# The scales of the split units: sums of magnitudes on ScalarE in place of maxima on VectorE, an exponentials' table loaded first, and a new listed order

## The chip, the cores and the metric

One core of one Trainium2 chip runs the program. The metric is the device time of one execution in microseconds (us); lower is better. Times before and after are medians of several runs, and each version was also executed once with the hardware profiler.

Engines are named as in the profile: PE (TensorE, matmuls; PEld is its weight load), DVE (VectorE), ACT (ScalarE), POOL (GpSimd), SP (SyncE, which here issues all the DMAs).

## The reference

Attention with two kinds of masks, and then one feed-forward block over all tokens:

```
scores = q @ k^T / sqrt(64)                      # 8 batches, 8 heads, 576 positions
mask   = window of 32 (heads 0-3), or every 4th of 128 back (heads 4-7)
attn   = softmax(scores where mask, else -1e9)
x      = (attn @ v) as 4608 tokens x 512
h      = x @ w_in                                # 512 -> 2048
g      = h * tanh(softplus(h))                   # Mish
out    = g @ w_out                               # 2048 -> 512
```

All inputs and the output are float32.

## The kernel before

The work is cut into 16 units of 288 tokens: unit u is half u % 2 of batch u // 2. A unit is loaded (`loads`, `loads_v`), prepared (`prep`), attended in four pairs of heads (`scores_of_pair`, `scores`, `exps`, `transpose_p`, `values`), and goes through the two layers (`ff1` or, from unit 4 on in pairs of units, the seven products `s_p1` to `s_p7`; then `gate` and `ff2`).

To keep float32 accuracy with float16 products, numbers are split: a value, multiplied by a power of two, is written as a high float16 part and a low one that holds the rest, and three products are added up. The weights are split at the start (`w_load`, `w_max`, `w_scale`, `w_words`, `w_split`). Units 0 to 2 are "direct": their attention is in float32, and only v's maximum is needed. Units 3 to 15 are "split": q, k and v are split as well, and `prep` makes the powers of two for them.

For a split unit, `prep` has these steps (each `yield` ends one):

1. POOL clears `m` (L497), and DVE takes the maximum magnitude of each partition of q (`amax`, L327), then of the two k tiles, then of the two v tiles: five reductions into the columns of `m`.
2. `over_partitions` (L336): one PE matmul of `m` with ones, which gives every partition the same sum over the partitions of each column.
3. DVE joins pairs of columns (L516) and cuts the result to a power of two (`pow2_scales`, L321 to L323).
4. ACT scales q (L541), writes the high parts of q (L544), k (L548) and v (L564); POOL (L551) and DVE (L554, L568) subtract for the low ones.

[...] Exponentials (L689, L695) and Mish (L947, L1028) lie in different tables, so an ACT_TABLE_LOAD stands wherever the two follow each other.

Nothing is scheduled on the chip. `ORDER` is a list written out ahead, in which a name such as `pr3` is the next step of `prep(3)`, and a number behind it names the buffer or the PSUM bank that the step takes. The program runs through the list, and each engine gets its instructions in that order. The four banks (pairs of 512 columns in PSUM) are shared by all products. `kw` entries are matmuls of zeros (L1081) that keep PE at work while it has nothing else to do. `ol` (`open_late`) gives back the buffers of the weights' loading and takes others in their place, which POOL clears (L712, L714); `wf` (`w_forms`, L871 to L877 on POOL) makes combinations of the weights for the pairs of units; `mr` makes the masks (L305).

Of the kernel before, what the change touches and what calls it, by code (L numbers as in the profile page):

```python
# [45 lines left out]
tx0.1 tx0.1 wl0.2.1=1 va0.3=1 sp1.1=0 tp0.0=1 wp0.3.1 xa0.1=1 tp0.0=0 wp0.3.0 tx0.3=2 sc1.1=0 lv1 wp0.3.1 wp0.3.0 tx0.3
kw9=3 va0.0=1 va0.0 kw11=3 tx0.3 va0.0=0 sp1.0=0 sc1.0=2 wl0.1.1=0 tx0.3 wm0.2.1=0 ww0.2.1 va0.2=2 va0.2 ex1.0 va0.2=1
ws0.2=1 ws0.2 tx0.0=2 tx0.0 tx0.2=0 tx0.2 tx0.0 tx0.0 ww0.2.1 sp1.2=1 wm0.1.1=0 ww0.1.1 sp1.3=2 sc1.3=3 tx0.2 tx0.2
ff0.1=3 ff0.6=0 ff0.6 wl0.1.0=3 wm0.1.0=0 sc1.2=1 ww0.1.0 ww0.2.0 ws0.1=1 ws0.1 ff0.1 wp0.2.1 ex1.3 pr1 ex1.2 ww0.1.1
xa1.1=2 ex1.1 wp0.2.0 wp0.2.0 tp1.3=2 tp1.3=0 fs0 ff0.0=1 ff0.6=0 ld2 ff0.0 ff0.0=1 ff0.1 ff0.7=2 pr1=0 pr1 gt0.0=0  # L50
ff0.7 ff0.7 wp0.2.1 wp0.1.1 va1.3=1 ww0.1.0 tp1.0=0 tp1.0=1 va1.3 va1.3=0 tp1.1=2 tp1.1=0 wp0.1.1 kw8=3 va1.0=0 va1.0
wp0.1.0 va1.0=1 tp1.2=2 tp1.2=1 lv2 ff0.5=3 pr2 va1.1=1 tx1.3=2 tx1.3 ff0.4=0 ff0.4 xa1.0=3 gt0.3=1 va1.1 wl1.3.1=2
va1.1=0 wl1.2.0=1 wm1.2.0 wp0.1.0 ww1.2.0 pr2=1 gt0.3 ff0.4=2 tx1.3 tx1.3 ff0.5 tx1.0=0 pr2 wl1.2.1=0 ff0.2=2 wm1.2.1
tx1.0 tx1.1=1 tx1.0 ff0.2 ww1.2.1 wm1.3.1 ww1.3.1 tx1.1 tx1.1 tx1.0 va1.2=0 ws1.2=1 ff0.5 gt0.2=2 xa2.1=4 ww1.3.1
ff0.3=3 va1.2 va1.2=1 tx1.2=0 ff0.2=0 sp2.1=2 ws1.2 wl1.3.0=3 wm1.3.0 ww1.3.0 tx1.2 tx1.2 sc2.1=3 sp2.3=1 sc2.3=2 tx1.2
ex2.3 ws1.3=0 ws1.3 ex2.1 ff0.3 ww1.3.0 ff1.2=0 ff1.6=1 wp1.3.1 wp1.3.1 ww1.2.1 xa2.0=0 tp2.1=2 tp2.1=0 ff1.2 gt0.2
gt0.0 va2.1=2 ff0.3 wp1.3.0 wp1.3.0 wp1.2.1 wp1.2.1 ff1.6 ww1.2.0 ff1.7=3 ff1.7 fs1 ff1.6=2 ff1.2=1 ff1.7 gt1.3=3 va2.1
va2.1=0 wl1.0.1=2 wm1.0.1 gt1.3 ff1.3=1 ff1.3 ww1.0.1 ff1.3 tp2.3=0 sp2.2=3 gt0.1=4 gt0.1 tp2.3=1 sc2.2=0 ff1.1=1
wl1.0.0=3 gt1.1=5 ff1.0=2 ff1.0 wm1.0.0 ww1.0.0 wl1.1.0=0 ff1.1 ff1.0=2 wp1.2.0 gt1.1 ff1.1 va2.3=0 va2.3 ws1.0=2
wp1.2.0 ws1.0 ex2.2 wm1.1.0 sp2.0=1 sc2.0=1 va2.3=1 ex2.0 fo0.2.0=2 fo0.2.1 ww1.1.0 ww1.0.1 ff1.5=3 ff1.5 gt1.0=6  # L60
tx2.1=0 gt1.0 wl1.1.1=1 ff1.4=1 wm1.1.1 tx2.1 wp1.0.1 ff1.4 ff1.4=0 ff1.5 fs2 fo0.2.2 ww1.1.0 tx2.1 tx2.1 ww1.1.1
wf1.1=1 fo0.2.3 fo0.2.3=0 lv3 tp2.0=1 ww1.1.1 wp1.0.1 tp2.2=3 ww1.0.0 fo0.3.0 ws1.1=0 ws1.1 tp2.2=0 va2.2=3 tp2.0=1
va2.0=1 va2.0 va2.0=0 gt1.2=7 fo0.3.1 gt1.2 fo1.2.0=0 tx2.0=1 wp1.1.0 fo1.2.1 fo1.2.2 wp1.1.0 fo1.2.3 wp1.1.1 wp1.1.1
fo0.2.3 va2.2 va2.2=0 tx2.2=3 wp1.0.0 tx2.2 fo0.3.2 wp1.0.0 fo0.3.3 tx2.2 fo0.3.3=1 tx2.2 fo1.2.3=0 fo1.3.0 fo1.3.1
tx2.3=2 ol wf0.0=2 wf0.0 mr ld3 tx2.0 pr3 pr3 wf0.0=0 pr3 pr3=3 wf0.0 pr3 fo1.3.2 tx2.3 wf1.1 fo0.3.3 wf1.1=2 wf1.1
wf0.0 fo0.0.0=3 wf1.1 fo1.2.3 tx2.3 fo1.3.3 fo0.0.1 fo0.0.2 pr3 pr3 fo0.0.3 fo1.3.3=1 tx2.0 fo1.3.3 pr3 pr3 pr3 sp3.1=2
pr3 fo0.0.3=0 pr3 sp3.2=1 sc3.1=3 ex3.1 ld4 sp3.0=0 fo0.1.0 fo0.1.1 sc3.0=2 sc3.2=1 xw4.0=2 fo1.0.0=2 fo1.0.1 fo1.0.2
fo0.0.3 wf0.1=1 fo1.0.3 lv4 wf0.1 ex3.0 wf0.1=0 sp3.3=0 tp3.1=0 wf0.1 tp3.0=1 fo0.1.2 wf0.1 fo1.0.3=1 fo0.1.3 ff2.3=1
fo1.1.0 fo1.1.1 ex3.2 tp3.0 tp3.0=0 sc3.3=0 ex3.3 tp3.3=1 pr4 wf1.0=2 tp3.1 tp3.1=1 ff2.0=0 ff2.0 ff2.0=1 fo1.1.2
va3.0=0 pr4 pr4 fo0.1.3=0 wf1.0 xa3.1=1 pr4=3 pr4 ff2.3 wf1.0=0 wf1.0 fo0.1.3 wf1.0 fo1.1.3 tp3.3 fo1.1.3=0 ff2.5=3  # L70
# [1067 lines left out]
```

## Time and profile before

| | before |
|---|---|
| median of 3 timed runs | 885.92 us (885.57 to 889.34) |
| profiled execution | 883.43 us, its span 881.7 us |
| PE busy | 856.6 us (97%) |
| DVE busy | 682.4 us (77%) |
| ACT busy | 609.7 us (69%) |
| POOL busy | 190.2 us (22%) |
| granted PE clock, mean | 0.996 |

The span is the time from the first instruction to the last; the execution has 1.7 us around it. A busy share is an average over the span: stages with different limits lie in it. In the views, a row names the line, the engine, the operation, and what it writes and reads (out<-in); "idle before" is the time that the engine stood before it, and what ended it. A wait is put down to the event that came last.

### The profile page before, as it was taken

What the parts mean: (1) busy time and instruction counts of PE and PEld (TensorE: products, weight loads), DVE (VectorE), ACT (ScalarE), POOL (GpSimd) and SP (SyncE); (2) the same over time, 40 slices, a digit from 0 to 9 for tenths busy, and PEclk for the clock granted to TensorE, in tenths of its full rate; (3) what the DMA queues carried; (4) which work ended last, traced back from release to release, by engine and by line L of the source; (5) the groups of instructions that cost most, each with busy time, mean ns of one, the idle gap of its engine ahead of it and who ended that gap; (6) DMA issues with size and microseconds to landing.
All of it is one profiled execution on the core that took longest, in us unless ns stands there. A gap on an engine that the chain in (4) does not pass through costs nothing.

```text
span 881.7 us, 21314 instructions
## 1 busy us (share of the span) xinstructions
PE 856.6 (97%) x8920; PEld 689.4 (78%) x8924; DVE 682.4 (77%) x960; ACT 609.7 (69%) x853; POOL 190.2 (22%) x218
## 2 busy tenths in 40 slices
PE   9999996999999999999999999999999999999998
PEld 8687884778777778877888778877788778887776
DVE  6999995899998979669887899896987788633310
ACT  3787973566887689578976689748875688536521
POOL 1000106715445110351024010431024110220000
PEclk9999998999999999999999999999999999999999
DMA  7953432565788975766766777677867763655200
GB/s 239 307 185 114 153 123 71 169 157 114 186 168 196 219 199 154 166 158 207 201 142 140 220 185 168 136 170 199 205 132 178 182 204 70 134 114 188 97 25 31
DMA packets 210865, 141.20 MB, mean 160 GB/s; under 512 B 151376, under 2 KB 195920, under 8 KB 210768
## 3 DMA queue, kind: packets, MB, share of 16 engines
q1 hardware_dynamic: 210768, 139.83, 61.5%
q8 instruction: 70, 1.15, 0.5%
q14 instruction: 27, 0.22, 0.1%
HBM read 93.06 MB, written 16.78 MB: 125 GB/s over the span
## 4 chain that ended last, share of the span: by engine, by line
PE 56%; DVE 13%; ACT 4%; issue 3%; DMA 3%; POOL 1%; SPq 0%; DVEq 0%; ACTq 0%; POOLq 0%
PE b L1052 27%; PE b L937 24%; PE b L778 2%; DMA w<-wd 2%; PE b L624 2%; DVE m L327 2%; DVE g L1042 1%; DVE sb L648 1%; DVE sb L656 1%; DVE nm L654 1%; DVE p L739 1%; DVE w L922 1%; ACT k L548 0%; DVE w L796 0%; ACT p L737 0%
## 5 line engine op out<-in xcount | busy, mean ns | idle before, releaser
L1052 PE MATMUL b<-g,w 128*128 128x288 f16 x3072 | 391.5, 287 | 0.2 <-DVE xs L796 0.2
L1052 PEld LDWEIGHTS <-w 128*128 128x128 f16 x3072 | 297.7, 98 | 75.9 <-DVE xs L796 0.3
L937 PEld LDWEIGHTS <-w 128*128 128x128 f16 x2016 | 194.8, 98 | 52.3 <-DMA w<-wd 3.1
L937 PE MATMUL b<-xf,w 128*128 128x288 f16 x1440 | 210.3, 286 | 1.9 <-DMA w<-wd 1.9
L1066 ACT ACTIVATE y<-b,fo 128x288 f32<-128x288 f32 x60 | 44.2, 744 | 90.4 <-PE b L1052 66.7
L1042 DVE SCALAR_TENSOR_TENSOR g<-hm,sg,g 128x1152 f16<-128x1152 f32 x64 | 90.6, 1421 | 17.9 <-ACT g L1040 17.8
L1025 PE MATMUL b<-xf,w 128*128 128x288 f16 x768 | 99.1, 286 | 2.7 <-DVE xs L796 1.2
L1025 PEld LDWEIGHTS <-w 128*128 128x128 f16 x768 | 74.1, 98 | 22.8 <-issue 2.1
L551 POOL TENSOR_TENSOR q<-qn,q 128x288 f16<-128x288 f32 (+1 forms) x39 | 45.5, 1198 | 172.9 <-ACT q L544 172.9
L1040 ACT ACTIVATE g<-hm,sg 128x1152 f16<-128x1152 f32 x64 | 79.9, 1252 | 1.1
L947 ACT ACTIVATE hm<-hm,fs 128x576 f32<-128x576 f32 x72 | 54.2, 769 | 15.7 <-DVE hm L998 7.1
L937 PE MATMUL b<-w,w 128*128 128x288 f16 x288 | 64.3, 286 | 0.0
L695 ACT ACTIVATE sb<-sb,ln_p 96x768 f32<-96x768 f32 (+3 forms) x52 | 46.4, 895 | 17.3 <-DVE sb L656 17.0
L656 DVE TENSOR_TENSOR sb<-sb,nm 96x768 f32<-96x768 f32 (+4 forms) x64 | 56.6, 884 | 2.2
L739 DVE TENSOR_TENSOR p<-sb,p 96x768 f16<-96x768 f32 (+3 forms) x52 | 51.1, 984 | 4.0 <-ACT p L737 3.8
L654 DVE TENSOR_REDUCE nm<-sb 96x6 f32<-96x768 f32 (+4 forms) x64 | 48.8, 762 | 1.8
L922 DVE TENSOR_TENSOR w<-w,w 72x1024 f16<-72x1024 f32 (+3 forms) x27 | 29.4, 1092 | 22.3 <-ACT w L920 22.3
L778 PEld LDWEIGHTS <-pT 128*128 128x128 f16 (+3 forms) x1092 | 39.3, 98 | 3.2 <-issue 1.0
L737 ACT CAST p<-sb 96x768 f16<-96x768 f32 (+3 forms) x52 | 41.0, 793 | 0.6
L910 POOL TENSOR_TENSOR w<-xs,w 72x1024 f32<-72x1024 f32 (+1 forms) x6 | 12.9, 2145 | 128.4 <-DVE xs L796 128.4
L937 PE MATMUL b<-xg,w 128*128 128x288 f16 x288 | 39.2, 286 | 0.0
L871 POOL TENSOR_TENSOR hm<-w 128x1024 f32<-128x1024 f16 x8 | 18.8, 2345 | 93.1 <-DVE g L1042 79.9
(173 smaller groups left out, 1194.8 us busy)
## 6 DMA issues: line engine op xcount, KB each, us to landing
w<-wd SPq DMA_DIRECT2D x84, 512.0 KB
qn<-in_qT SPq DMA_DIRECT2D x16, 576.0 KB
out_T<-y SPq DMA_DIRECT2D x64, 144.0 KB
raw<-in_w_in SPq DMA_DIRECT2D x16, 512.0 KB
raw<-in_w_out SPq DMA_DIRECT2D x16, 512.0 KB
vn<-in_v SPq DMA_DIRECT2D x48, 128.0 KB
wd<-hm SPq DMA_DIRECT2D x32, 128.0 KB
knd<-in_kdT SPq DMA_DIRECT2D x16, 208.0 KB
```

The costliest lines, as they stand in the source:

```text
L551: nc.gpsimd.tensor_tensor(lo, x, hi, op=ALU.subtract)
L654: nc.vector.tensor_reduce(nm[:nq, :, j:j + n], x, axis=AX.X, op=ALU.max, negate=True)
L656: nc.vector.tensor_tensor(blocked(sb, c0, n, w), x, nm[:nq, :, j:j + n].unsqueeze(3).broadcast_to([nq, 2, n, w]), op=ALU.add)
L695: nc.scalar.activation(x, x, AF.Exp, bias=ln_p[:nq])
L739: nc.vector.tensor_tensor(lo, src, hi, op=ALU.subtract)
L778: nc.tensor.matmul(avv[:, h, j], pp[:nk, c:c + P], vv[vi][:nk, j, hh, :], start=(i == 0), stop=(i == 2))
L937: nc.tensor.matmul(o[:, h, :HT], t[:, c, wi, h * P:(h + 1) * P], form_of(p, x, c, xi), skip_group_check=True, start=start and n == 0, stop ...
L947: nc.scalar.activation(o, src, AF.Mish, scale=U[2 * p]["fs"][:, j:j + 1])
L1025: nc.tensor.matmul(ph[:, h, :HT], w1[j][c // WIDE][:, c % WIDE, wi, k * P:(k + 1) * P], x_of(d, xi, c), start=(n == 0), stop=(n == len(seq ...
L1040: nc.scalar.activation(g[:, 0], m, AF.Identity, scale=sg)
L1042: nc.vector.scalar_tensor_tensor(g[:, 1], m, sg, g[:, 0], ALU.mult, ALU.subtract)
L1052: nc.tensor.matmul(po[:, :HT], w2[:, e, j, wi, k * P:(k + 1) * P], d["g"][j][:, gi, k, :], start=(j == 0 and n == 0), stop=(j == NCH - 1 a ...
```

## The change

Four things are different.

- `prep` of a split unit no longer takes maxima. `magnitudes` runs on ACT: the function Abs over the tile, divided by 1024, with the sum along the row put out (`accum_out`). The values themselves go to a place that is written later anyway (the high halves of q, k and v). A sum of magnitudes is no smaller than the largest, so it bounds the values as well.
- The sum over partitions by one matmul is replaced by `largest`: PE transposes the six columns, DVE takes the maximum of each row, DVE sets the six on the diagonal of a small matrix, and PE multiplies it with ones. This puts two PE steps in a unit's preparation where there was one. `m` is float32 for split units, and `pow2_scales` gets other constants.
- An exponential of one column is the first thing that ACT does, so its table is loaded ahead of everything else.
- `ORDER` is a new list (2355 entries; 2329 before): 26 more steps for the 13 split units, and the others in another sequence. `kw` has 249 matmuls of zeros in all, 269 before; ahead of the first weights' scales 136, before 226.

```
+MANY = 1024.0
...
-kw16=0 kw16=0 kw16=0 kw16=0 kw16=0 kw16=0 kw16=0 kw16=0 kw16=0 kw16=0 kw16=0 kw16=0 kw16=0 kw2=0 ws0.0=0 ws0.0 wp0.0.0
...
-    def pow2_scales(m, f, s):
+    def pow2_scales(m, f, s, tiny=TINY, by=2.0 ** -SPLIT_EXP):
...
-        nc.vector.tensor_scalar(f, f, TINY, 2.0 ** -SPLIT_EXP, ALU.max, ALU.mult)
+        nc.vector.tensor_scalar(f, f, tiny, by, ALU.max, ALU.mult)
...
+    def magnitudes(o, i, unused):
+        nc.scalar.activation(unused, i, AF.Abs, scale=1.0 / MANY, accum_out=o)
+
+    def largest(m, n, u):
+
+        t = single(u)[:n, :P]
+        nc.tensor.transpose(t, m[:, :n], ident)
+        yield
+        top = pool.tile([8, 1], F32, name="top", bufs=3)
+        nc.vector.tensor_reduce(top[:n], t, axis=AX.X, op=ALU.max)
+        on_diagonal = pool.tile([8, 8], BF16, name="dg", bufs=3)
+        nc.vector.tensor_scalar(on_diagonal[:n, :n], ident[:n, :n], top[:n], None, ALU.mult)
+        yield
+        o = single(u)[:, :n]
+        nc.tensor.matmul(o, ones_b[:n].broadcast_to([n, P]), on_diagonal[:n, :n], start=True, stop=True)
+        yield
+        return o
...
-        m = pool.tile([P, 6], BF16, name="m", bufs=3)
+        m = pool.tile([P, 6], BF16 if d["direct"] else F32, name="m" if d["direct"] else "mm", bufs=3)
...
-        amax(m[:, 4:5], qn)
+        magnitudes(m[:, 4:5], qn, q2[:, 0])
...
-            amax(m[:, 2 + i:3 + i], x)
+            magnitudes(m[:, 2 + i:3 + i], x, k2[:, 0, ksl[i]])
...
-        for x, o in ((vn, m[:, 0:1]), (vdn[:kd], m[:kd, 1:2])):
-            amax(o, x)
+        for x, o, y in ((vn, m[:, 0:1], vh[:, 0]), (vdn[:kd], m[:kd, 1:2], vdh[:kd, 0])):
+            magnitudes(o, x[:, :, :, :D].rearrange("p j h d -> p (j h) d"), y[:, :, :, :D].rearrange("p j h d -> p (j h) d"))
...
-        mr = yield from over_partitions(m, 6, u)
+        mr = yield from largest(m, 6, u)
...
-        pow2_scales(m3, f, s)
+        pow2_scales(m3, f, s, TINY / MANY, MANY * 2.0 ** -SPLIT_EXP / 2)
...
+    first = const.tile([P, 1], F32, name="first")
     with tc.manual_schedule(engines=None):
+        nc.scalar.activation(first, ln_p, AF.Exp)
```

How the new list moves instructions shows at three places. The first is the start, on DVE: `raw` is a weight tile as loaded, `w` its place, and `wm` the maximum that the first scales are made of. Before:

```order
L409 TENSOR_SCALAR w_125<-w_125 128x1024
L411 SCALAR_TENSOR_TENSOR raw_76<-raw_76,w_125 128x1024
L412 SCALAR_TENSOR_TENSOR raw_76<-raw_76 128x1024
L409 TENSOR_SCALAR w_119<-w_119 128x1024
L411 SCALAR_TENSOR_TENSOR raw_77<-raw_77,w_119 128x1024
L412 SCALAR_TENSOR_TENSOR raw_77<-raw_77 128x1024
L409 TENSOR_SCALAR w_118<-w_118 128x1024
L411 SCALAR_TENSOR_TENSOR raw_78<-raw_78,w_118 128x1024
L412 SCALAR_TENSOR_TENSOR raw_78<-raw_78 128x1024
L384 TENSOR_REDUCE wm_417<-b_72 128x1
```

After (line numbers are those of the changed kernel, 20 higher here):

```order
L429 TENSOR_SCALAR w_119<-w_119 128x1024
L431 SCALAR_TENSOR_TENSOR raw_76<-raw_76,w_119 128x1024
L432 SCALAR_TENSOR_TENSOR raw_76<-raw_76 128x1024
L429 TENSOR_SCALAR w_118<-w_118 128x1024
L431 SCALAR_TENSOR_TENSOR raw_77<-raw_77,w_118 128x1024
L432 SCALAR_TENSOR_TENSOR raw_77<-raw_77 128x1024
L404 TENSOR_REDUCE wm_323<-b_72 128x1
```

Two weight tiles stand ahead of the first scales instead of three. The second place is POOL where unit 3, the first split unit, begins: `p` and `pT` are tiles that `open_late` takes, `hm` a working tile of the weight forms, `m_d` and `m_r` the masks, and `m` (now `mm`) the columns of `prep(3)`. Before:

```order
L712 MEMSET p_1982 96x2048
L714 MEMSET pT_1984 128x1328
L871 TENSOR_TENSOR hm_140<-w_118 128x1024
L874 TENSOR_TENSOR hm_140<-hm_140 128x256
L875 TENSOR_TENSOR hm_140<-hm_140 128x256
L876 TENSOR_TENSOR hm_140<-hm_140 128x256
L877 TENSOR_TENSOR hm_140<-hm_140 128x256
L305 COPY m_d<-m_s 72x288
L305 COPY m_d<-m_s 72x416
L305 COPY m_r<-m_r 96x384
L497 MEMSET m 128x6
```

After:

```order
L732 MEMSET p_1906 96x2048
L734 MEMSET pT_1908 128x1328
L517 MEMSET mm 128x6
L891 TENSOR_TENSOR hm_139<-w_118 128x1024
L894 TENSOR_TENSOR hm_139<-hm_139 128x256
```

The clearing of unit 3's columns moved ahead of the weight forms and of the masks. The third place is the same one on the engine that goes over unit 3's tiles. On DVE before, from the last weight split (`w` from `raw` and its scale `ws`) to the columns' join:

```order
L424 SCALAR_TENSOR_TENSOR w_126<-raw_79,ws_1571,w_126 128x512 x2
L1058 TENSOR_SCALAR fo<-h_o,f 128x1 x2
L1064 TENSOR_SCALAR y_88<-b_72,fo 128x288
L327 TENSOR_REDUCE m<-qn 128x1
L327 TENSOR_REDUCE m<-knp 128x1
L327 TENSOR_REDUCE m<-knd 128x1
L327 TENSOR_REDUCE m<-vn 128x1
L327 TENSOR_REDUCE m<-vdn 104x1
L883 TENSOR_TENSOR hm_138<-hm_140,hm_138 128x1024
L516 TENSOR_REDUCE m_2026<-b_75 128x3
```

On ACT after, behind the last weight part:

```order
L1048 ACTIVATE hm_139<-b_72,fs 128x576
L844 CAST xf_133<-b_75 128x4x72
L1060 ACTIVATE g_162<-hm_139,sg 128x1152
L849 CAST xf_133<-b_75 128x4x72
L844 CAST xf_136<-b_73 128x288
L844 CAST xf_133<-b_72 128x4x72
L901 CAST hm_138<-hm_140 128x1024
L1086 ACTIVATE y_89<-b_74,fo 128x288
L345 ACT_TABLE_LOAD
L345 ACTIVATE q_1916,mm<-qn 128x1152
L345 ACTIVATE k_1931,mm<-knp 128x640
L345 ACTIVATE k_1931,mm<-knd 128x832
```

The passes over unit 3's tiles moved from DVE to ACT, with a table load ahead of them: the Mish passes just before (L1048) had their own table in place. The passes over v's two tiles follow. In the whole program the new order has 60 table loads for 44, and 11 of them stand directly ahead of magnitudes.

More of the change, by code (lines that the diff above doesn't have):

```diff
@@ L46 @@
[L46 to L70, printed above, removed]
@@ L186 @@
[L186 to L189 removed]
+xa0.0=0 wl0.0.1=0 wm0.0.1=0 ww0.0.1 ww0.0.1 wl0.0.0=1 wm0.0.0=0 ww0.0.0 ww0.0.0 kw16=0 kw16=0 kw16=0 kw16=0 kw16=0
@@ new lines @@
+zc4.3=3 tp10.3=1 va10.3=2 zc4.3 zc4.3 va10.3 tp10.1=0 zl4.13=1 ld12 zt5.0.0=2 zt5.1.0=4 pr11 lv12 zd4.3 va10.3 zd4.3
+fo7.1.3 zg4.3 va10.1=3 xw11.0=2 ex11.0 ze4.3 zg4.3 sp11.3=2 tx2.0 ze4.3 sp11.2=1 tp11.0=0 tp11.0 va10.1 zf4.3 va10.1
+fo8.0.0=3 ex11.1 tp11.1=1 zf4.3 zt5.0.3=0 tp11.1 sc11.3=3 tp11.1=1 gt8.3=7 tp11.0=0 gt8.3 pr12 fo8.0.1 gt9.2=2
+zt5.1.0=1 sc11.2=2 fo8.2.0=0 fo8.2.1 fo8.2.2 ex11.3 fo8.2.3 fo8.0.2 fo8.0.3 zt5.1.0 zl5.1=2 ex11.2 zt5.1.0 va11.0=2
+gt9.2 va11.1=1 tp11.3=1 tp11.3 fo8.2.3=0 fo8.3.0 tp11.2=0 tp11.2 fo8.0.3=1 va11.1 va11.0 va11.0 va11.1 fo8.3.1 fo8.3.2
@@ new lines @@
+pr14 fo10.1.3 zt6.0.3=0 gt11.2 fo11.0.0=2 zl6.2=0 fo10.1.3=1 fo10.1.3 gt11.3=3 gt11.3 zt6.0.2=0 zt6.0.3=0 zt6.0.3
+zt6.0.3 fo10.3.1 va13.2=3 fo10.3.2 fo10.3.3 fo10.3.3=0 pr14 pr14 pr14 zt6.0.2=1 zt6.0.2 va13.3=1 va13.3 fo11.0.1 va13.2
+fo11.0.2 xw13.1=1 zt6.0.2 fo10.3.3 fo11.0.3 fo11.0.3=1 pr14 fo11.0.3 va13.3 va13.2 zt6.1.1=1 zt6.1.1=0 sp14.1=0
+sc14.1=1 sp14.2=1 zt6.1.1 ex14.1 sp14.0=3 ld15 sc14.2=0 fo11.1.0 fo11.1.1 fo11.1.2 fo11.1.3 sc14.0=3 zt6.1.3=1
+fo11.1.3=0 pr15 zt6.1.1 zt6.1.2=5 zt6.1.2=1 fo11.2.0=0 fo11.2.1 fo11.2.2 zt6.1.3=0 fo11.2.3 fo11.2.3=1 za6.0=1 zt6.1.2
@@ new lines @@
+va15.3 gt12.3=3 gt12.3 xw15.1=0 va15.3 va15.2 va15.2 zt7.1.1=0 zt7.0.3=1 zt7.1.1=0 zt7.0.3 fo12.2.3 zt7.1.1 zt7.0.3
+zt7.1.2=5 zt7.1.1 fo12.0.0=3 fo12.0.1 fo12.0.2 fo12.0.3 fo12.2.3=1 za7.0=1 fo12.3.0 fo12.3.1 fo12.0.3=0 fo12.0.3
+fo12.2.3 zt7.1.3=1 fo12.3.2 zt7.1.3=1 fo12.1.0 zt7.1.3 zt7.1.3 zt7.1.2=0 za7.0=2 fs14 fo12.3.3 fo12.3.3=0 fo12.1.1
+zc7.0=2 fo13.1.3=1 zt7.1.2 zt7.1.2 fo12.1.2 zd7.0 zb7.0=0 fo12.1.3 zc7.0 zc7.0 zl7.2=1 zb7.0=0 zd7.0 ze7.0 zl7.4=2
+fo13.1.3 ze7.0 ze7.0 zg7.0 zg7.0 zg7.0 fo12.1.3=1 gt15.0=1 zl7.3=0 zc7.1=2 zb7.1=0 gt15.0 zf7.0 zf7.0 gt14.0=0 za7.1=3
@@ L190 @@
+zf7.3 fo15.0.3 fo14.2.1 fo15.3.0 gt14.3=2 gt14.3 fo15.1.0 fo15.1.1 fo14.0.0=3 fo14.0.1 gt14.2=3 gt14.2 fo14.2.2
+fo14.0.2 fo15.1.2 fo15.1.3 fo14.2.3 fo14.2.3=1 fo15.1.3=0 fo14.0.3 fo14.3.0 fo14.3.1 fo15.1.3 fo14.2.3 fo15.3.1
+fo15.3.2 fo15.3.3 fo14.3.2 fo14.0.3=0 fo14.0.3 fo14.1.0 fo15.3.3=1 fo15.3.3 fo14.1.1 fo14.1.2 fo14.1.3 fo14.1.3=0
+fo14.1.3 fo14.3.3 fo14.3.3=1 fo14.3.3
 """.split()
```

253 lines of the change are left out of this document (130 added, 123 removed).

## The prediction, as put on record

> **What bounds the kernel now.** I read the page's totals first, then PE's waits, then busy time by stage, then the order of time at the two places where PE stands. The page's first lines:
>
> ```profile
> span 881.7 us, 21314 instructions
> PE 856.6 (97%) x8920; PEld 689.4 (78%) x8924; DVE 682.4 (77%) x960; ACT 609.7 (69%) x853; POOL 190.2 (22%) x218
> ```
>
> PE is busy for 856.6 of 881.7 us, so all the standing on PE is 25.1 us: nothing that only relieves another engine can give more. The profiled execution took 883.43 us, 1.7 us around its span; the median of the three timed runs is 885.92, so 2.5 us above it. The sum below is a difference against the profiled execution and is put on the median. The waits by engine and line (total us, times, longest):
>
> ```profile
> PE b L336 <- DVE m L327: 9.2, 2, 8.5
> ...
> DVE m L327 <- POOL m L497: 8.1, 1, 8.1
> ...
> DVE m L327 <- DMA vdn<-in_vd: 4.1, 3, 2.5
> ```
>
> One wait of 8.5 us is a third of PE's standing. It is the L336 matmul (the maxima made common to all partitions) of the first split unit, 3. Busy time by stage (start:end, length, then PE, PEld, DVE, ACT, POOL busy):
>
> ```profile
> 140.00:160.00 20.00, 11.51 (x84) 8.63 (x82) 10.93 (x16) 9.07 (x13) 13.20 (x22) 0.83 0.42 120
> ...
> 150.60:881.70 731.10, 720.46 (x7501) 578.07 (x7501) 554.33 (x743) 505.19 (x674) 169.00 (x181) 1.00 0.64 158
> 160.00:280.00 120.00, 116.49 (x1325) 93.63 (x1324) 113.79 (x156) 86.80 (x116) 57.03 (x58) 1.00 0.67 158
> 280.00:760.00 480.00, 477.18 (x5126) 384.13 (x5124) 402.12 (x541) 365.31 (x490) 100.35 (x112) 1.00 0.70 173
> ```
>
> After the wait, PE is idle for 731.1 - 720.46 = 10.6 us: 3.5 up to 280, where DVE is at 95%, 2.8 in the 480 us after that, and the rest in what remains up to the end. Ahead of it the start counts. In order of time (start, length, engine, line):
>
> ```profile
> 6.18 1.28 ACT L366 ACT_TABLE_LOAD   x1 [6.18 <-DMA raw<-in_w_in]
> 7.47 1.14 ACT L366 ACTIVATE w<-raw 128x1024 f32<-128x1024 f32 x1
> ...
> 8.64 0.69 DVE L409 TENSOR_SCALAR w<-w 128x1024 int32<-128x1024 int32 x1 [7.66 <-ACT w L366]
> ...
> 15.64 1.06 PE L377 MATMUL b<-w,ones 128*128 128x512 bf16 x3 [0.46 <-DVE w L409]
> ```
>
> The table load waits for the first weights and delays DVE by its 1.28 us. DVE then fills its time, as the page's slices of 22 us show (busy tenths, 9 for 90% or more), up to its last weight split in the seventh, and that end and what follows decide when unit 3 may begin:
>
> ```profile
> DVE  6999995899998979669887899896987788633310
> ```
>
> ```profile
> 135.07 1.40 DVE L424 SCALAR_TENSOR_TENSOR w<-raw,ws,w 128x512 f16<-128x512 f32 x2
> ...
> 145.47 1.35 DVE L327 TENSOR_REDUCE m<-qn 128x1 bf16<-128x1152 f32 x1 [8.14 <-POOL m L497]
> ...
> 151.51 0.16 DVE L516 TENSOR_REDUCE m<-b 128x3 f32<-128x6 f32 x1
> ```
>
> ```profile
> 132.98 1.80 POOL L712 MEMSET p<- 96x2048 f16 x1 [21.97 <-DMA knp<-in_kT]
> ...
> 137.61 1.20 POOL L714 MEMSET pT<- 128x1328 f16 x1
> ...
> 145.34 0.10 POOL L497 MEMSET m<- 128x6 bf16 x1
> ```
>
> ```profile
> 135.29 0.44 PE L814 MATMUL b<-ident,xs 72*128 72x72 f32 x4
> 135.57 3.10 PE L1052 MATMUL b<-g,w 128*128 128x288 f16 x24
> ...
> 150.61 0.17 PE L336 MATMUL b<-m,ones 128*128 128x6 bf16 x1 [8.49 <-DVE m L327]
> ```
>
> Call the end of the last split T: 135.07 + 1.40 = 136.5. POOL clears four tiles (132.98 to 138.8), then does one unit of weight forms and the masks before it clears m at 145.34; only then do the maxima run, and PE goes on at 150.61, T + 14.1.
>
> **The change, part by part.** *Table load first.* It leaves the chain of the first weights: DVE starts 1.28 us earlier, so T goes to 135.2, since the same weight words and splits stand ahead of it. It costs nothing: ACT has nothing to do until 6.18. That two weight tiles instead of three are now made ready before the first scales lets PE begin earlier, but DVE does the same sum of work by T, so I count it at nothing; without a busy DVE it would be worth up to the third tile's 3.1 us of PE.
>
> *Unit 3's chain.* In the new order exactly as many 288-column products stand ahead of its step on PE as before, so the whole gain of this stage is the time at which that step ends. POOL now clears m right behind the four tiles, at T + 5.9 (they last 132.98 to 138.8 now, plus 0.1), since the first of these waits for the split that has become the last. ACT has eight instructions and a table load between its last weight part and the first magnitudes; at its mean of 609.7/853 = 0.71 us these take 6.4 us, so the magnitudes begin at about T + 6.4. Their price is taken from the nearest rows, passes of ACT over the same tiles:
>
> ```profile
> L541 ACT ACTIVATE qn<-qn,s 128x1152 f32<-128x1152 f32 x13 | 16.3, 1256 | 5.2 <-DVE s L323 5.1
> ...
> L548 ACT ACTIVATE k<-knd,s 128x832 f16<-128x832 f32 x7 | 6.8, 976 | 0.0
> ...
> L548 ACT ACTIVATE k<-knp,s 128x640 f16<-128x640 f32 x7 | 5.8, 824 | 0.0
> ...
> L564 ACT ACTIVATE vh<-vn,s 128x768 f16<-128x768 f32 x13 | 12.1, 928 | 0.0
> ...
> L564 ACT ACTIVATE vdh<-vdn,s 104x1024 f16<-104x1024 f32 x7 | 8.0, 1140 | 0.0
> ...
> L786 ACT ACTIVATE den<-b,pf 96x6 f32<-96x6 f32 x24 | 8.3, 346 | 8.4 <-PE b L778 8.4
> ...
> L1058 DVE TENSOR_SCALAR fo<-h_o,f 128x1 f32<-128x1 f32 x12 | 2.3, 202 | 0.0
> ...
> L654 DVE TENSOR_REDUCE nm<-sb 96x2 f32<-96x192 f32 x12 | 4.1, 342 | 0.0
> ```
>
> Together 1.26 + 0.98 + 0.82 + 0.93 + 1.14 = 5.1 us. No row shows a sum written out at an instruction's end; it lies between nothing and a whole smallest instruction, 0.35 us, five times 1.7; I take nothing, because the rows above already read a scale from memory, which these don't. Then PE's transpose (0.17), DVE's maximum over 128 columns (0.34, the row of 192 columns) and the small diagonal (0.20), and PE's last matmul (0.17): 0.9. The step ends at T + 6.4 + 5.1 + 0.9 = T + 12.4 = 147.6 instead of 150.6: **-3.0 us**. Bounds: -4.5 (magnitudes begin at T + 5.9 and take a fifth less) to 0 (1.7 for the sums, and 1.3 for an ACT that waits for PE on the way).
>
> *The other twelve units.* PE gets a transpose and a small matmul where one matmul was. The L814 row has four transposes in 135.29 to 135.57, 0.07 each; alone in the queue one would cost the 0.17 of L336. I take 0.1: **+1.2 us** (0.8 to 2.0). The products that stand between the two (12 to 36, at 3.10/24 = 0.13 us) cover DVE's two small steps of 0.54; without them it would be 0.54 a unit, 6.5 in all.
>
> *What DVE loses and ACT gains.* The maxima of one unit:
>
> ```profile
> L327 DVE TENSOR_REDUCE m<-qn 128x1 bf16<-128x1152 f32 x13 | 17.5, 1346 | 8.1 <-POOL m L497 8.1
> ...
> L327 DVE TENSOR_REDUCE m<-vn 128x1 bf16<-128x768 f32 x16 | 15.1, 944 | 0.0
> ...
> L327 DVE TENSOR_REDUCE m<-vdn 104x1 bf16<-104x1024 f32 x8 | 9.7, 1215 | 4.1 <-DMA vdn<-in_vd 4.1
> ...
> L327 DVE TENSOR_REDUCE m<-knd 128x1 bf16<-128x832 f32 x7 | 7.1, 1010 | 0.0
> ...
> L327 DVE TENSOR_REDUCE m<-knp 128x1 bf16<-128x640 f32 x7 | 5.7, 812 | 0.0
> ...
> L695 ACT ACT_TABLE_LOAD x19 | 24.4, 1283 | 0.3
> ```
>
> That is 5.3 us for a unit of the second half (a little less for the first), 13 times about 68; DVE gets back 13 x 0.54 = 7, so it loses some 61 of 682. ACT gains 13 x 5.1 = 66 and, with 60 table loads in the new order for 44, 16 x 1.28 = 20.5: from 610 to 696. None of this is on PE's path by itself. From 280 to 760 us nine of the thirteen units are prepared: ACT rises from 365 to at most 365 + 46 + 20.5 = 432 of 480, 90%; DVE falls from 84% to about 75%. The engine with the least room changes, at about the height DVE had (84% there, 95% before 280). I take back half of the 3.5 us that PE stands between 160 and 280, -1.7, since DVE loses some 15 of 114 us there, and add 1.1 for the fuller ACT: **-0.6 us** (bounds -5 and +2).
>
> A switch of tables in the trace:
>
> ```profile
> 182.54 1.28 ACT L1028 ACT_TABLE_LOAD   x1
> 183.83 0.74 ACT L1028 ACTIVATE hm<-b,fs 128x576 f32<-128x576 f32 x1
> ```
>
> The next instruction starts 1.29 us behind the load, so a switch costs its 1.28. [...]
>
> Sum: -3.0 + 1.2 - 0.6 = **-2.4 us**: a span of 879.3 instead of 881.7, and 883.5 against the median of 885.92. That is 0.3%, and 0.5% (4.4 us) is about what a measurement can tell.
>
> **The rivals.** *The room on DVE is worth more.* The new order could use it in all places where PE stands after unit 3's step, 3.5 + 2.8 us. If two thirds of that goes (4.2), and the transposes hide down to 0.9: -3.0 + 0.9 - 4.2 = -6.3, 879.6 us. For it: L336 waited for DVE or POOL, not for PE. Against: the 2.8 us over 480 is already little, and ACT now lies in the same path.
>
> *ACT's queue holds up PE's banks* (slower). DVE waited 4.1 us in three places for v's loads, and nothing of PE's was urgent behind that. Now ACT waits there, in order, and behind the magnitudes are queued the copies and Mish passes that empty the product banks, for which PE waits. If each of twelve units costs PE 0.75 us (half of the 4.1/3 = 1.4 of such a wait), it is +9.0 - 2.4 = +6.6, 892.5 us. It decides from 6.8/12 = 0.57 us a unit on. Against: ACT itself waits for PE in the present trace, as it did 8.4 us for the sums of the L786 row, so evictions have room.
>
> *The stage of unit 3 ends no earlier:* ACT comes late or sums cost 0.35 each, and the first term goes to 0: +1.2 - 0.6, 886.5 us.
>
> **How the numbers follow.** Forecast -2.4: 0.35. No gain at unit 3: 0.15; both lie within 0.5%, so same 0.50. DVE's room: 0.33, faster. ACT's queue: 0.17, slower. The bounds added give -4.5 + 0.8 - 5 = -8.7, 877 us, and 0 + 2.0 + 2 = +4.0, 890; the range reaches a little into the slower case and leaves most of it out: 877.5 to 891.
>
> **What would show it.** Right: DVE's first weight word near 7.4 us; the diagonal's matmul near 147.6; magnitudes of 5.1 us a unit; 60 table loads of 1.28; PE idle behind that matmul of some 10 us. Wrong: a first term outside -4.5 to 0; PE waiting more than 7 us in all for ACT's copies or for the transposes; magnitudes well over 1.3 us for qn, or a gap behind the loads.

## The result, and the profile after

The changed kernel takes 892.02 us (median of 6 runs, 891.22 to 892.83); the kernel before took 886.61 us beside it (6 runs, 885.57 to 889.34). The ratio is 1.0058, 95% interval 1.0042 to 1.0074: slower, by 5 us, where 2.4 us less was forecast. The profiled execution took 891.22 us, with a span of 889.4 after 881.7. So by the two profiles the kernel is 7.7 us slower and by the medians 5.4: the profiled execution of before lies 3.2 us under its median, that of after 0.8. What follows compares profiles, and a difference against the kernel before is known to some 2 us. The load of the engines, as the page gives it:

```profile
PE 862.5 (97%) x8914; PEld 691.3 (78%) x8917; DVE 634.3 (71%) x921; ACT 687.3 (77%) x1000; POOL 174.8 (20%) x218
```

The work moved as the change says: DVE is busy for 48 us less, ACT for 78 us more. PE, which had nothing taken away, is busy for 5.9 us longer, and stands for 26.9 us, 1.8 more than before.

The first stage came out much shorter. In order of time, the start and then unit 3's step (the lines are 20 higher than before; L345 is the pass over the magnitudes, L350 and L358 are PE's two new steps):

```profile
6.31 1.15 ACT L386 ACTIVATE w<-raw 128x1024 f32<-128x1024 f32 x1 [4.09 <-DMA raw<-in_w_in]
7.50 0.69 DVE L429 TENSOR_SCALAR w<-w 128x1024 int32<-128x1024 int32 x1 [6.51 <-ACT w L386]
11.37 1.06 PE L397 MATMUL b<-w,ones 128*128 128x512 bf16 x3 [0.73 <-DVE w L429]
...
130.77 1.40 DVE L444 SCALAR_TENSOR_TENSOR w<-raw,ws,w 128x512 f16<-128x512 f32 x2
138.01 0.10 POOL L517 MEMSET mm<- 128x6 f32 x1
138.14 1.16 ACT L345 ACTIVATE q<-qn 128x1152 f16<-128x1152 f32 x1 [0.93 <-POOL mm L517]
142.68 0.19 ACT L345 ACTIVATION_READ_ACCUMULATOR vdh<-vdn 104x1 f32 x1
143.01 0.27 PE L350 MATMUL b<-ident,mm 128*6 128x128 f32 x1 [0.73 <-ACT vdh L345]
143.90 0.16 PE L358 MATMUL b<-dg,ones 6*128 6x6 bf16 x1 [0.62 <-DVE dg L355]
```

T, the end of the last weight split, is 130.77 + 1.40 = 132.2 (before 136.5). The step's last product, which began at 150.61, now begins at 143.90, 6.7 us earlier. So everything was lost behind it, where 745.5 us follow in place of 731.1. The busy time there, as a whole and in the two stretches that the prediction used:

```profile
143.90:889.40 745.50, 725.75 (x7513) 580.04 (x7512) 509.19 (x705) 576.03 (x809) 153.54 (x183) 1.00 0.62 154
160.00:280.00 120.00, 113.40 (x1247) 90.04 (x1246) 97.73 (x141) 101.64 (x143) 47.71 (x53) 0.99 0.69 157
280.00:760.00 480.00, 473.03 (x5028) 378.53 (x5023) 358.13 (x506) 409.22 (x578) 82.87 (x109) 1.00 0.67 170
```

PE stands for 745.5 - 725.75 = 19.75 us there, 9.1 more than before: 6.6 in place of 3.5 up to 280, 7.0 in place of 2.8 up to 760. DVE's load has fallen from 95% to 81% and from 84% to 75%, ACT's has risen from 72% to 85% and from 76% to 85%. And PE's busy time itself grew by 5.3 us. What PE waits for:

```profile
PE b L798 <- ACT y L1086: 3.5, 1, 3.5
PE b L350 <- ACT vdh L345: 2.5, 2, 1.7
PE b L798 <- ACT hm L1048: 2.4, 1, 2.4
PE b L1045 <- DVE sb L668: 2.4, 1, 2.4
PE b L350 <- ACT sb L715: 1.3, 1, 1.3
PE b L358 <- ACT hm L1048: 1.3, 1, 1.3
```

Before, DVE's maxima (9.2, one wait of 8.5) and a few DMAs (1.9) led this list, and no wait for ACT was over 0.7 us. Now five of the six longest end with ACT: a copy that empties a bank (L1086), a Mish pass (L1048), the magnitudes. They are few and long. One of them in order of time, at unit 5's step:

```profile
188.24 1.28 ACT L345 ACT_TABLE_LOAD   x1
...
189.53 1.17 ACT L345 ACTIVATE q<-qn 128x1152 f16<-128x1152 f32 x1
...
192.40 1.28 ACT L1048 ACT_TABLE_LOAD   x1
193.70 1.37 ACT L1048 ACTIVATE hm<-b,fs 128x576 f32<-128x576 f32 x2
...
194.49 0.68 PE L798 MATMUL b<-vdh,pT 104*128 104x65 f16 x17 [2.42 <-ACT hm L1048]
```

ACT leaves Mish's table for the magnitudes and goes back to it. PE's next products need a bank that the Mish pass at 193.70 empties, and it comes behind both loads, 2 x 1.28 us. The groups of ACT show what each part costs (busy us, mean ns of one):

```profile
L345 ACT ACTIVATE q<-qn 128x1152 f16<-128x1152 f32 x13 | 15.1, 1165 | 2.7 <-POOL mm L517 2.7
L345 ACT ACT_TABLE_LOAD x11 | 14.1, 1283 | 0.2
...
L345 ACT ACTIVATION_READ_ACCUMULATOR k<-knp 128x1 f32 x13 | 2.5, 189 | 0.0
```

From here on there were three explanations. A: what was put into ACT's queue is late for PE's banks, by its table loads (A1) or by its passes (A2). B: PE's own two steps stand in its queue and wait. C: the new order is the worse one.

### The profile page after: what moved, and what is told of

Read it like the earlier page. It is cut to its first block, busy times and chain, and to the rows that moved or that the text cites. A ratio compares the mean times of both kernels' runs of the same rounds, so it can differ in the third digit from the quotient of the medians.

```text
span 889.4 us, 21433 instructions
## 1 busy us (share of the span) xinstructions
PE 862.5 (97%) x8914; PEld 691.3 (78%) x8917; DVE 634.3 (71%) x921; ACT 687.3 (77%) x1000; POOL 174.8 (20%) x218
## 4 chain that ended last, share of the span: by engine, by line
PE 69%; DVE 9%; ACT 9%; issue 6%; DMA 3%; POOL 1%; SPq 1%; DVEq 0%; ACTq 0%; POOLq 0%
PE b L1072 33%; PE b L957 26%; PE b L1045 4%; PE b L798 3%; PE b L644 3%; DMA knp<-in_kT 1%; DVE nm L674 1%; DVE g L1062 1%; ACT L345 1%; DVE sb L668 1%; ACT k L345 1%; DVE sb L676 1%; DVE raw L431 1%; DVE p L759 1%; ACT g L1060 1%
## 5 line engine op out<-in xcount | busy, mean ns | idle before, releaser
L1062 DVE SCALAR_TENSOR_TENSOR g<-hm,sg,g 128x1152 f16<-128x1152 f32 x64 | 93.6, 1466 | 45.6 <-ACT g L1060 45.5
L1086 ACT ACTIVATE y<-b,fo 128x288 f32<-128x288 f32 x60 | 44.0, 741 | 58.0 <-PE b L1072 47.3
L571 POOL TENSOR_TENSOR q<-qn,q 128x288 f16<-128x288 f32 (+1 forms) x39 | 38.8, 1023 | 164.7 <-ACT q L564 164.7
L967 ACT ACTIVATE hm<-hm,fs 128x576 f32<-128x576 f32 x72 | 53.6, 769 | 17.0 <-DVE hm L1003 8.4
L715 ACT ACTIVATE sb<-sb,ln_p 96x768 f32<-96x768 f32 (+3 forms) x52 | 46.3, 896 | 15.0 <-DVE sb L676 14.8
L798 PEld LDWEIGHTS <-pT 128*128 128x128 f16 (+3 forms) x1092 | 39.5, 98 | 10.1 <-issue 7.6
L940 ACT CAST w<-w 72x1024 f16<-72x1024 f32 (+3 forms) x29 | 24.6, 847 | 16.7 <-POOL w L931 7.9
```

Of the source, the lines that this page charges most:

```text
L715: nc.scalar.activation(x, x, AF.Exp, bias=ln_p[:nq])
L798: nc.tensor.matmul(avv[:, h, j], pp[:nk, c:c + P], vv[vi][:nk, j, hh, :], start=(i == 0), stop=(i == 2))
L967: nc.scalar.activation(o, src, AF.Mish, scale=U[2 * p]["fs"][:, j:j + 1])
L1062: nc.vector.scalar_tensor_tensor(g[:, 1], m, sg, g[:, 0], ALU.mult, ALU.subtract)
L1086: nc.scalar.activation(o, src, AF.Identity, scale=fo)
```

## The experiments

Each kernel was timed against the kernel before on the same chip, whose median lay between 884.95 and 886.11 us in these series; so ratios are compared, each with an interval of about 0.0015 to either side (1.3 us; 1.9 us for the difference of two). A ratio of 0.001 is 0.89 us.

**The table first, alone.** The kernel before with

```diff
+    first = const.tile([P, 1], F32, name="first")
     with tc.manual_schedule(engines=None):
+        nc.scalar.activation(first, ln_p, AF.Exp)
```

> The kernel before, its old listed order and its maxima on VectorE, with the exponentials' table loaded first and nothing else. In the changed kernel PE's first weight product starts at 11.37 us and not at 15.64, and the last weight split ends at 132.2 us and not at 136.5: 4.3 us earlier. If that is the table alone and PE's idle end of the first stage follows it, this kernel takes about 882.3 us (886.6 - 4.3). The forecast's first term (the table is worth 1.3 us) gives 885.3 us. If the earlier start comes from the new order and the table brings nothing, 886.6 us.

Measured: 885.52 us (882.25 to 890.27, 12 runs), ratio 1.000 (0.9985 to 1.0015): nothing that can be measured. That is near the second and the third number, which the uncertainty doesn't part, and far from 882.3. In order of time ACT does begin earlier, but T moves little:

```profile
6.19 1.13 ACT L366 ACTIVATE w<-raw 128x1024 f32<-128x1024 f32 x1 [3.96 <-DMA raw<-in_w_in]
...
134.34 1.40 DVE L424 SCALAR_TENSOR_TENSOR w<-raw,ws,w 128x512 f16<-128x512 f32 x2
```

T is 135.7 instead of 136.5. So the early start of the changed kernel comes mostly from the order, which makes two weight tiles ready before the first scales and not three (the last experiment measures it).

**Maxima on VectorE in the new order.** The changed kernel with

```diff
-        nc.scalar.activation(unused, i, AF.Abs, scale=1.0 / MANY, accum_out=o)
+        amax(o, i)
...
-        pow2_scales(m3, f, s, TINY / MANY, MANY * 2.0 ** -SPLIT_EXP / 2)
+        pow2_scales(m3, f, s)
```

> The changed kernel with its new order, its table first and its two steps on PE, but with VectorE's maxima in place of ScalarE's magnitudes (66 us back from ScalarE to VectorE, and 12 of the 16 added table loads gone). Theory A (what stands in ScalarE's queue keeps PE's banks from being emptied; it cost the changed kernel about 14.4 us behind unit 3's step): most of that comes back, less some 2 us at unit 3's step, which waits for VectorE again: 879 to 884 us. Theory B (PE waits at its two new steps, whoever fills the column of sums): the waits stay, 890 to 894 us. Theory C (the new order itself is the worse one): 888 us or more.

Measured: 927.82 us, ratio 1.0474 (1.0452 to 1.0497). A and B missed; C's "888 us or more" takes it in, without having expected such a size. In this order the maxima cost 37 us more than the magnitudes. Its waits on PE, and unit 3's step in order of time:

```profile
PE b L350 <- DVE mm L329: 19.6, 8, 5.6
```

```profile
143.91 1.20 DVE L329 TENSOR_REDUCE mm<-vdn 104x1 f32<-104x1024 f32 x1
...
145.89 3.04 PE L1072 MATMUL b<-g,w 128*128 128x288 f16 x12 [4.90 <-DVE y L1084]
...
149.72 0.16 PE L358 MATMUL b<-dg,ones 6*128 6x6 bf16 x1 [0.63 <-DVE dg L355]
```

The order fits the engine that it was written for. With the maxima back on DVE, PE waits for them at eight of the steps, 19.6 us in all, and at unit 3 also for a copy (L1084) that stands behind them in DVE's queue and empties a bank, 4.9 us. It also gives the price of the change at unit 3: the last product begins at 149.72 with maxima and at 143.90 with magnitudes, in the same order. C, as "the order is worse whoever does the work", can't be told from this kernel, and A's number had taken for granted that the order suits DVE too.

**The same passes without the loads.** The changed kernel with

```diff
-        nc.scalar.activation(unused, i, AF.Abs, scale=1.0 / MANY, accum_out=o)
+        nc.scalar.activation(unused, i, AF.Identity, scale=1.0 / MANY, accum_out=o)
```

> The changed kernel with ScalarE's pass in a function whose table is always there (identity with the sum read out, so the absolute value is left out): the same 66 us of passes in the same places, but 48 table loads and not 60. Theory A1 (within A, the loads do the harm: each stops ScalarE for 1.28 us ahead of a copy that PE waits for): 6 us or more come back, 886 us or less. Theory A2 (the passes themselves do it): 2 us or less come back, 890 us or more. Theories B and C: 891 to 892 us.

Measured: 875.95 us, ratio 0.9885 (0.987 to 0.9901). That is 0.0173 or 15.3 us less than the changed kernel, for 12 loads of 1.283, 15.4 us. In its trace the loads at exponentials (L715) are 21 for 16, those at Mish (L967, L1048) 24 for 30, and at L345, where the changed kernel has 11, none is listed: 12 fewer. A1 holds; B and C, by which next to nothing should have happened, don't explain it. The sums are signed here, so this kernel tells what the passes cost and computes something else.

**The loads without most of the passes.**

```diff
+        few = (slice(None),) + (slice(0, 1),) * (len(i.shape) - 1)
-        nc.scalar.activation(unused, i, AF.Abs, scale=1.0 / MANY, accum_out=o)
+        nc.scalar.activation(unused[few], i[few], AF.Abs, scale=1.0 / MANY, accum_out=o)
```

> The changed kernel with its 60 table loads and all its places, but each of the magnitudes' passes reads one element (or one of each head's) in a partition and not the whole row (most of the sum is left out): about 50 us of ScalarE's 66 are gone, the loads stay. Theory A1 (the loads): 889 us or more. Theory A2 (the passes): 6 us or more come back, 886 us or less. Theories B and C: 890 us or more.

Measured: 881.20 us, ratio 0.9945 (0.9927 to 0.9962), 10.0 us less than the changed kernel. This is A2's number, beside A1's in the last experiment: each alone gives most of the loss back.

**Neither.** Both edits together, identity over one element:

> Identity in one element (or one of each head's) of a partition: neither the 12 loads nor about 50 us of the passes (sum and absolute value left out). Without the loads alone 16.1 us came back, with short passes alone 10.8. If ScalarE's queue has one debt that either can pay (what remains of the delays is none of its), both together give little more than the missing loads: 872.5 to 876 us. If each holds up PE at places of its own, the two add up: about 865 us.

Measured: 876.77 us, ratio 0.9895 (0.9881 to 0.991), no better than without the loads alone, a little above the range for one debt and far from the 865 us of two. So it is one debt. Without the loads, the passes cost nothing that can be measured: ACT has room for 50 us more, but not at these places for 50 us and the loads.

**Squares: the whole computation, without the loads.** The changed kernel with

```diff
-        nc.scalar.activation(unused, i, AF.Abs, scale=1.0 / MANY, accum_out=o)
+        nc.scalar.activation(unused, i, AF.Square, accum_out=o)
...
         nc.vector.tensor_reduce(m3, mr.rearrange("p (a b) -> p a b", b=2), axis=AX.X, op=ALU.max)
+        nc.vector.tensor_scalar(m3.bitcast(I32), m3.bitcast(I32), 0.5, float(127 << 22), ALU.mult, ALU.add)
-        pow2_scales(m3, f, s, TINY / MANY, MANY * 2.0 ** -SPLIT_EXP / 2)
+        pow2_scales(m3, f, s)
```

> The changed kernel with ScalarE's pass in squares and not in absolute values, nothing left out: the squares' sum bounds the square of the largest element, and one small VectorE instruction per unit halves its exponent. 48 table loads and not 60, the passes as long as before. If the loads did the harm (theory A1; identity in their place took 875.95 us), 875.5 to 878 us: identity's time and 13 VectorE instructions of about 0.2 us, most of them beside other work. If the time of the kernel with identity came from something else than its missing loads, 885 us or more.

Measured: 876.94 us (875.96 to 877.58), ratio 0.9899 (0.9884 to 0.9915): as expected, and a kernel that beats both, by 9 us and 14 us. The same place as above in it (its lines are one higher from L537 on):

```profile
188.60 1.15 ACT L345 ACTIVATE q<-qn 128x1152 f16<-128x1152 f32 x1
...
191.34 1.34 ACT L1049 ACTIVATE hm<-b,fs 128x576 f32<-128x576 f32 x2
192.17 1.63 PE L799 MATMUL b<-vdh,pT 104*128 104x65 f16 x48
```

No load stands there, the Mish pass comes at 191.34 and not 193.70, and PE doesn't wait at all.

**One step on PE.** The changed kernel with `largest` cut to

```diff
-        t = single(u)[:n, :P]
-        nc.tensor.transpose(t, m[:, :n], ident)
         yield
...
+        mb = pool.tile([P, 6], BF16, name="mb", bufs=3)
+        nc.vector.tensor_copy(mb, m)
         yield
         o = single(u)[:, :n]
+        nc.tensor.matmul(o, ones_b.broadcast_to([P, P]), mb, start=True, stop=True)
```

> The changed kernel with its 60 loads and its passes, but the reduction over the partitions is one step on PE, at the place of the second one (a product of ones with the columns copied to bf16, which gives a looser bound: the sum over the partitions, not the largest). PE no longer transposes the columns, where it waited for ScalarE or VectorE for about 5 us in all. Theory B (the first of the two steps is where the time went): 885 to 887 us. Theory A (ScalarE's queue is late for PE's banks whatever reads its sums): 889 to 892 us, as the wait turns up at the next bank.

Measured: 891.03 us, ratio 1.0054 (1.004 to 1.0069), 0.4 us less than the changed kernel, within the uncertainty: B is out. PE's waits in it:

```profile
PE b L794 <- ACT y L1082: 3.7, 1, 3.7
PE b L1068 <- ACT y L1082: 2.7, 2, 2.4
PE b L794 <- ACT hm L1044: 2.4, 1, 2.4
```

The long waits for ACT at the values' products (L794 here, L798 there) are where they were, and in place of the transposes PE waits at the next bank (L1068).

**Squares in the old order.** The kernel before, its one step on PE kept, and k's and v's maxima replaced like q's:

```diff
-        amax(m[:, 4:5], qn)
+        nc.scalar.activation(q2[:, 0], qn, AF.Square, accum_out=m[:, 4:5])
```

> The kernel before with its old listed order and its one step on PE, ScalarE's squares in the places where VectorE's maxima stood (the columns in bf16, a looser bound), no added table load, the exponentials' table not loaded ahead. If taking 61 us from VectorE is what gains, and the new order only makes room for ScalarE's loads: 874 to 878 us. If the order has to fit the engine that does the work, as the new order with maxima on VectorE (927.8 us) suggests: ScalarE's passes in old places hold up PE's copies, 884 us or more. The forecast's estimate for the relief of VectorE (0.6 us and 3.0 at unit 3's step) gives 882 us.

Measured: 912.99 us, ratio 1.030 (1.0275 to 1.0324). Its first wait on PE:

```profile
PE b L340 <- ACT vdh L335: 16.4, 7, 8.3
```

The mirror image of the maxima in the new order: a relief of DVE as large (it is busy for 623.0 us), without one added load, costs 27 us where the order is written for the other engine. In this program a relief of DVE gains nothing by itself; the order has to fit it.

**As much plain work, spread.** The kernel with squares and one more pass in each split unit:

```diff
+        nc.scalar.activation(q2[:, 0], qn, AF.Square)
         magnitudes(m[:, 4:5], qn, q2[:, 0])
```

> The kernel with squares (876.9 us, 48 loads) and one more ScalarE pass of the queries in each of its 13 split units, 128x1152, about 1.16 us, straight ahead of the first pass, with no sum read and its output written over: 15.1 us more in ScalarE's queue, where the changed kernel has 12 more loads of 1.283 us, 15.4 us. If the loads cost by the time they hold the queue: 887 to 893 us. If a load costs by something of its own (ScalarE's pipeline is emptied around it), and plain work of the same length does not: 880 us or less.

Measured: 881.75 us, ratio 0.9961 (0.9946 to 0.9975), 5.5 us more than squares alone, for 15.1 us of work. Neither number of the expectation: plain work spread over 13 units costs two fifths of what the loads cost (14.1 us against squares). That could be the load itself or its place. Compared instruction by instruction, the changed kernel has 17 loads that the kernel with identity lacks, 11 ahead of magnitudes and 6 on the way back to Mish, and lacks five that stand ahead of exponentials there. Five of the 17 are these five, moved forward to the magnitudes; the other twelve are all in the steps of units 5, 6, 10 and 11, six pairs.

**As much plain work in those places.** The kernel with squares and 12 more passes, one ahead of the magnitudes there, and one ahead of the next Mish:

```diff
+    def filler(u, part):
+        if (u, part) in ((5, "q"), (5, "v"), (6, "q"), (6, "k"), (10, "q"), (11, "v")):
+            nc.scalar.activation(U[u]["q2"][:, 0], U[u]["qn"], AF.Square)
+            owed.append(u)
```

> The kernel with squares (876.9 us, 48 loads) and 12 more ScalarE passes of 1.16 us, 13.9 us in all, each at a place where the changed kernel has a load that this one lacks: ahead of the magnitudes of units 5 (queries, values), 6 (queries, keys), 10 (queries) and 11 (values), and ahead of the next Mish behind each. In one pass per unit, 15.1 us, they cost 4.8 us. If what costs is time in ScalarE's queue at these places, where banks wait for the next Mish or copy: 887 to 891 us. If a table load costs by something else than the time it takes: 883 us or less, as for the spread passes.

Measured: 886.33 us, ratio 1.0004 (0.9993 to 1.0015), 9.3 us more than squares alone, for 13.9 us of work. A little under the range that was expected, and far from the other. Unit 5's step once more, with the two passes (L351, L357) in the places of the loads:

```profile
188.69 1.15 ACT L351 ACTIVATE q<-qn 128x1152 f16<-128x1152 f32 x1
...
192.69 1.15 ACT L357 ACTIVATE q<-qn 128x1152 f16<-128x1152 f32 x1
193.74 1.34 ACT L1066 ACTIVATE hm<-b,fs 128x576 f32<-128x576 f32 x2
194.51 1.62 PE L814 MATMUL b<-vdh,pT 104*128 104x65 f16 x48 [2.08 <-ACT hm L1066]
```

PE's products begin at 194.51, against 194.49 with the loads and 192.17 without: time in the queue, at that place, is what counts. The three stretches with these units (start:end, length, then PE, PEld, DVE, ACT, POOL busy, granted clock), of the changed kernel, of squares, and of squares with the 12 passes. They are cut at the same times, so in the third the kernels are up to 14 us apart in their work:

```profile
185.00:205.00 20.00, 17.59 (x233) 13.57 (x231) 14.81 (x31) 19.79 (x28) 6.00 (x5) 0.91 0.76 145
255.00:275.00 20.00, 16.52 (x187) 13.10 (x186) 15.57 (x21) 18.43 (x30) 9.98 (x8) 1.00 0.71 169
455.00:505.00 50.00, 46.51 (x485) 36.66 (x484) 31.19 (x45) 36.64 (x56) 12.98 (x16) 0.97 0.59 145
```

```profile
185.00:205.00 20.00, 19.91 (x264) 16.01 (x262) 19.29 (x36) 19.27 (x30) 10.17 (x8) 1.00 0.76 162
255.00:275.00 20.00, 20.00 (x234) 16.08 (x232) 15.04 (x27) 15.21 (x26) 12.52 (x13) 1.00 0.86 164
455.00:505.00 50.00, 48.80 (x496) 38.82 (x495) 35.87 (x60) 38.69 (x60) 11.73 (x12) 1.00 0.62 163
```

```profile
185.00:205.00 20.00, 17.29 (x241) 13.70 (x240) 16.64 (x33) 19.73 (x28) 6.03 (x5) 1.00 0.82 160
255.00:275.00 20.00, 17.29 (x192) 13.49 (x190) 14.75 (x22) 18.13 (x33) 11.31 (x9) 1.00 0.75 163
455.00:505.00 50.00, 46.65 (x485) 37.17 (x482) 33.46 (x49) 38.93 (x59) 14.46 (x15) 1.00 0.63 164
```

PE stands for 9.4, 1.3 and 8.8 us in these 90 us. Over the whole stage behind unit 3's step it stands for 19.75, 9.23 and 17.51 us; the last is from

```profile
144.08:884.10 740.02, 722.51 (x7513) 578.63 (x7512) 510.72 (x718) 574.05 (x810) 155.43 (x183) 1.00 0.63 155
```

In the first stretch ACT is busy for 99%, 96% and 99%: full with the loads, with a little room without. What the loads cost beyond the 12 passes, 5 us, goes in part to their length (15.4 us for 13.9, a tenth of 9.3) and in part to the clock: it is below 1.00 in two of the stretches of the changed kernel and in none of the other two kernels, and PE is busy for 3.2 us longer behind unit 3's step than with the passes (725.75 against 722.51).

**Squares without the table first.** The kernel with squares without the two lines of the first experiment.

> The kernel with squares (876.9 us) without the table loaded first. In the old order the table first gave 0.3 us with 1.3 us of uncertainty. If the early start of the changed kernel (first weight product at 11.37 us and not 15.64) comes from the order alone, and the first pass of the words' maxima begins 1.16 us later behind the load, as in the kernel before: 877 to 878.2 us. If the table is what brings the start forward: 880 to 881.5 us.

Measured: 878.01 us, ratio 0.9915 (0.9899 to 0.993), 1.4 us more than with the table, an effect of the size of its uncertainty, and of the delay that it removes. PE's first weight product:

```profile
12.46 0.84 PE L397 MATMUL b<-w,ones 128*128 128x512 bf16 x2 [2.21 <-DVE w L429]
```

With the table first it begins at 11.30 in the kernel with squares, and in the kernel before at 15.64. T is 133.4 here, 132.2 with the table first, in the kernel with squares as in the changed one, and 136.5 before. So in the new order the table is worth 1.2 us of T, and the order brings the other 3.1 by itself.

## Why the prediction was wrong

**Table load first** (forecast: T 1.3 us earlier). T came 4.3 us earlier. The table's share was sized about right: 0.7 in the old order, without a measurable effect on the time, and 1.2 in the new one (last experiment). The step that failed here, in the kernel's favour, is the next sentence of the prediction: that two weight tiles are made ready instead of three was counted "at nothing", because DVE was to do "the same sum of work by T". It doesn't. From its first weight word to T, DVE before is busy for 122.0 of 127.8 us (8.64 to 136.47), after for 119.5 of 124.7 (7.50 to 132.17): 1.1 us from the earlier start, 2.4 from less busy time, 0.7 from less standing. Of the 2.4, 1.6 is work that now stands behind T (one pass L1042 of 1.4 and one L1058 of 0.2, by the line numbers of before); the rest is, on balance, instructions that took less time. PE's first product moved by 15.64 - 11.37 = 4.3 us, which is the first pass's 1.16 and the prediction's own alternative of 3.1.

**Unit 3's chain** (forecast -3.0, from -4.5 to 0). Measured -6.7: T is 3.0 earlier than forecast, and the step's last product begins at T + 11.7. The forecast's T + 12.4 is its end, 0.2 later than its begin, though it was compared with the begin at 150.61; in like terms -3.2 was forecast. The parts were near. The passes last 4.7 us, not 5.1; the sums that are read out cost 0.1 at the end of the chain, where nothing was taken. The passes begin at T + 6.0, not 6.4, but not for the reason given: ACT was through with its last weight part 3.4 us ahead of T, and with its eight instructions and the load by T + 5.0, and then waited for POOL's clearing, which was forecast at T + 5.9. So T + 6.4 came near by luck, and unit 3's own table load cost nothing. In the same order, magnitudes instead of maxima are worth 149.72 - 143.90 = 5.8 us here.

**The other twelve units** (+1.2, with the price of 6.5 "without them", the covering products). With one step and no transpose the time falls by 0.4 us, and the uncertainty is 1.9: nothing speaks against the term.

**What DVE loses and ACT gains** (-0.6, from -5 to +2). This is the step that put the forecast on the wrong side. The stage behind unit 3's step takes 745.5 us where 731.1 were needed, +14.4, of which 1.2 was forecast elsewhere. With squares the same stage takes 730.5 us:

```profile
144.00:874.50 730.50, 721.27 (x7513) 578.79 (x7512) 509.28 (x718) 562.52 (x798) 157.05 (x183) 1.00 0.64 157
```

That is 0.6 less than before; the prediction's other terms give -0.5 for it (+1.2 - 1.7), so within the 2 us to which it is known nothing speaks against them. So "add 1.1 for the fuller ACT" is the term that failed, and its size is 14 us by the medians and 15 by the profiles.

How it came to 1.1: the 16 loads were spread over the stage, 20.5 us in 480, and ACT then looked 90% full, as DVE had been. It became less full than that, 85% (over the whole program it gained 78 us, not 86, and DVE lost 48, not 61), and still cost far more. For a full engine holds up PE only where PE is waiting for its next instruction, and the loads aren't spread. Four of the 16 are in the kernel with squares too, and no cost of theirs is seen. The other 12 stand in pairs, away from Mish's table and back to it, in four units. Behind them in ACT's queue are passes that empty banks: in units 5 and 6 the Mish passes themselves (L1048), in unit 10 a copy (L1086 at 470.25, which ends the longest wait of the list). There they cost about their whole time: of the 15.0 us against squares, 10.5 are standing of PE and 4.5 its longer busy time, 3.4 of these by the clock (last section). Both facts were at hand, eleven loads directly ahead of magnitudes and Mish passes just before, and the prediction counted them instead of looking at what stands behind each.

What the loads stand between can be counted. In the changed kernel's trace ACT changes 22 times between magnitudes and Mish, with a load of 1.28 us at each (11 of them ahead of absolute values), 37 times between exponentials and Mish, with a load at each, and 24 times between magnitudes and exponentials, with none; with the one at the start these are the 60. In the kernel before, each of the 43 changes between exponentials and Mish had its load. None stands ahead of identity or squares in the magnitudes' places. Where a load for magnitudes was followed by exponentials, the exponentials needed none, in five places. So in these runs the table that was loaded for the absolute value served the exponentials too, and the one loaded for Mish didn't serve the absolute value.

**The slower rival** gave 892.5 us at 0.17, and 892.02 was measured. Its mechanism was half right: ACT's queue, in order, holds up PE's banks. What it priced was a wait of ACT for v's loads in each of twelve units, at 0.75 us; the trace has one wait of ACT's passes for a DMA, 1.2 us, and that for k. It was the table loads, in four units. The number agrees by chance. What the prediction held against this rival, that evictions have room because ACT waits for PE, failed too: in the changed kernel ACT waits for PE for 47.3 us at the copies (L1086), and still PE waits 3.5 us for one of them. Room on average is not room at a place. The faster rival, room on DVE that takes 4.2 us from the stage behind unit 3 (3.3 with its 0.9 for the transposes), isn't borne out: with squares, where nothing stands against it, the span is 7.2 us shorter than before, 6.6 by unit 3's step (144.00 for 150.61) and 0.6 behind it. By the medians squares gain 9 us, so it may be some 2 us there; not all of 3.3 was seen, and a part stays open.

Of the signs given for "wrong", two came: a first term outside its bounds, and PE waiting for more than 7 us for copies or transposes (in the list above the copy's 3.5 and the transposes' 2.5 and 1.3 make 7.3; its five rows that end with ACT make 11.0). Of those for "right", three came: DVE's first weight word at 7.50 us, 60 loads of 1.28, and passes of about the forecast length. Two did not: the last product near 147.6 (it began at 143.90), and some 10 us of standing behind it (19.75).
